# Two products of the identity ahead of each set of P's transposes, until the FFN begins

## The chip, the cores and the metric

The kernel runs on one core of one Trainium2 chip. A core has TensorE (matrix products, written into the banks of PSUM), VectorE, ScalarE, GpSimd and the queues that issue DMAs. The metric is the device time of one execution in microseconds. In the profile's rows TensorE is PE (its loads of weights PEld), VectorE is DVE, ScalarE is ACT, GpSimd is POOL, and SP issues DMAs.

## What is computed

Attention with a causal mask over blocks of 64 positions, for 8 batches of 8 heads with 576 positions of 64 columns, and behind it a feed-forward layer over the 4608 rows of the result:

```python
scores = scale * np.matmul(q, k.transpose(0, 1, 3, 2))
mask = (pos[:, None] // 64) >= (pos[None, :] // 64)
scores = np.where(mask, scores, -1000000000.0)
attn = np.exp(scores - scores.max(-1, keepdims=True))
attn = attn / (attn.sum(-1, keepdims=True) + 1e-09)
x = np.matmul(attn, v).transpose(0, 2, 1, 3).reshape(4608, 512)
h = x @ w_in                        # 512 x 2048
g = np.where(h >= 1, h, np.where(h <= -1, 0.0, (h + 1) ** 2 / 4))
out = g @ w_out                     # 2048 x 512
```

All of it is float32.

## The kernel before

**Split operands.** Operands are held in float32r, split into a high part and a low part (what the high part leaves over), so that a product is two or three products: scores are `qa`, `ka` and `qb`, `kb` (L482, L485), the FFN's first product is `wih` with `xh`, `wih` with `xl`, `wil` with `xh` (L770), its second is `gh` with two parts of w_out and `gl` with one (L794, L799). The parts of the weights are made while attention begins (`convert`, L156 to L189: ScalarE, VectorE and GpSimd in turn; VectorE's lines are L171, L174 and L177).

**Attention.** A pair of heads is one unit of work (`Pair`); there are 32, four to a batch. `scores` (L494) makes scores of 128 positions in a PSUM bank, VectorE takes their maximum (L505), ScalarE the exponential (L509), VectorE the reciprocal of the sum (L491, L492) and P (L515). `scores_last` (L518) does the same for the last 64 positions of both heads (L529 to L541). P must be transposed before it can be multiplied with V: `turn` (L556) and `turn_last` (L572) take a PSUM bank, transpose three or four pieces of 128x128 into it with TensorE (L554 for the first four pairs, L552 from the fifth on, when P has gone through a DMA first), and ScalarE copies the result out (L545). `weighted` (L587) multiplies it with V (L591); the result goes into `xh` and `xl` (L626, L627).

**Order of the work.** `attention_steps` (L663) is a generator of eight steps to a pair. The loop at L838 runs a step at a time, with pieces of the conversion of weights between them; from the 37th step on (`START` is 36, L830) it also runs a step of the FFN, and sets `banks["free"]` to False (L851). Until then `work_bank` (L80) takes every other bank from the four that the FFN's second product will use later. That written order is only the first word: a scheduler sets the order on each engine by priority and by its own estimate of times, and each engine takes its instructions in that order. So a set of transposes that waits for P holds back what stands behind it on TensorE.

Of the kernel before, what the change touches and what calls it, by code (L numbers as in the profile page):

```python
# [23 lines left out]
def block_attn_then_ffn(  # L24
# [9 lines left out]
    nc = tc.nc  # L34
# [25 lines left out]
    PLAIN = 2  # L60
    HOP = 1
    FAR = 2
    RAW = 2

    const = ctx.enter_context(tc.tile_pool(name="const", bufs=1))
# [12 lines left out]
    banks = {"free": True, "n": 0}  # L78

    def work_bank(name):  # L80

        banks["n"] += 1
        if banks["free"] and banks["n"] % 2:
            return ps_o.tile([P, 512], F32, tag="po", name=name)
        return ps_w.tile([P, 512], F32, tag="work", name=name)
# [4 lines left out]
    ident_r = const.tile([P, P], F32R, tag="ident", name="ident_r")  # L90
# [164 lines left out]
    class Pair:  # L255
# [4 lines left out]
        def __init__(self, b, hp):  # L260
# [6 lines left out]
            self.hop = b >= HOP  # L267
            self.raw = b >= RAW

            self.far = b >= FAR  # L270
            self.pr, self.nat = {}, {}
# [277 lines left out]
        def transposed(self, out, parts, c0, n):  # L549
# [3 lines left out]
            else:  # L553
                nc.tensor.transpose(out, src, ident)  # L554

        def turn(self, j, g):  # L556
            tiles = self.GROUPS[g]
            n = sum(t + 1 for t, _ in tiles) * P
            pr = self.pr.pop((j, g))
            ps = work_bank("ps_t")  # L560
            for c0 in range(0, n, P):
                self.transposed(ps[:, c0 : c0 + P], pr, c0, P)
            if g == 0:
                self.split(ps[:, :n], *self.pa[j])
            else:
                c0 = (g - 1) * P
                self.split(
                    ps[:, :n].rearrange("p (t c) -> p t c", c=P),
                    *(x[:, j, : n // P, c0 : c0 + P] for x in self.pb),
                )  # L570

        def turn_last(self):  # L572
            pr = self.pr.pop("last")
            ps = work_bank("ps_t")
            for c0 in range(0, SM, P):
                self.transposed(ps[:, c0 : c0 + P], pr, c0, P)
            self.split(
                ps[:, :SM].rearrange("p (t h c) -> p t h c", h=2, c=BLK),
                *(x[:, :, :, G1 - BLK :].rearrange("p h t c -> p t h c") for x in self.pb),
            )  # L580
            ps = work_bank("ps_t")
            self.transposed(ps[:BLK, :P], pr, SM, BLK)
            self.split(
                ps[:BLK, :P].rearrange("p (h c) -> p h c", h=2), *(x[:BLK] for x in self.pc)
            )
# [299 lines left out]
```

## Time and profile before

| | us |
|---|---|
| median of 3 runs | 1267.14 (1266.32 to 1267.73) |
| the profiled execution | 1269.69 |
| its span | 1267.9 |
| TensorE busy | 1200.1 |
| VectorE busy | 887.0 |
| ScalarE busy | 703.2 |
| GpSimd busy | 394.6 |

The span runs from the first to the last instruction of the profiled execution. Matmuls overlap, so the duration of one in a row is longer than the distance between two starts. "Idle" in square brackets of a row is the time in which the engine did nothing just before, with what ended it. PEclk is the granted clock of TensorE as a share of 2.4 GHz.

### The profile page before, as it was taken

Reading aid. Unit: us, or ns where it says so; the run is one execution under the profiler, and the core shown is the slowest. Engines: PE = TensorE matmul, PEld = TensorE weight load, DVE = VectorE, ACT = ScalarE, POOL = GpSimd, SP = SyncE. Lnnn points to the kernel's source line nnn. Section 1 sums busy time; section 2 is a strip of 40 time slices with the busy share of each in tenths; the row PEclk is TensorE's granted clock in tenths of the full one; section 3 lists DMA queues with packets and bytes.
Section 4 is the critical chain, followed back from the end, with each engine's and each line's share of the span. In section 5 each row is a group of like instructions: output and inputs, shape, how many; then the busy total and the mean of one; then the engine's idle time right before and its main releaser. Section 6 shows DMA issues by size and latency. Waiting matters only on the chain.

```text
span 1267.9 us, 20253 instructions
## 1 busy us (share of the span) xinstructions
PE 1200.1 (95%) x6280; PEld 998.8 (79%) x6280; DVE 887.0 (70%) x2188; ACT 703.2 (55%) x1827; POOL 394.6 (31%) x430
## 2 busy tenths in 40 slices
PE   5888889899999999999999999999999999999998
PEld 4666667678888888888888888888888888888886
DVE  8898877758777777777777777787777777322222
ACT  5787656646566655665656655566556555222222
POOL 3555655522222222222222222222222222222222
PEclk9888988999999999999999999999999999999999
DMA  5566666667888655555554655465556433422432
GB/s 158 167 176 215 203 228 197 217 198 237 260 273 266 215 162 158 154 175 163 156 162 145 187 157 152 138 189 153 160 154 190 137 128 118 132 87 98 133 100 100
DMA packets 185259, 215.43 MB, mean 170 GB/s; under 512 B 113840, under 2 KB 132272, under 8 KB 184384
## 3 DMA queue, kind: packets, MB, share of 16 engines
q1 hardware_dynamic: 185152, 214.14, 54.9%
q8 instruction: 50, 0.82, 0.3%
q14 instruction: 57, 0.47, 0.1%
HBM read 134.74 MB, written 31.98 MB: 131 GB/s over the span
## 4 chain that ended last, share of the span: by engine, by line
PE 69%; DVE 16%; ACT 6%; issue 5%; DMA 1%; POOL 1%; SPq 1%; ACTq 0%; POOLq 0%; DVEq 0%
PE ph L770 29%; PE po L794 15%; PE po L799 7%; PE ps_av L591 7%; PE ps_s L482 4%; ACT pr L509 3%; PE ps_s L485 3%; DVE t L780 2%; PE ps_t L552 2%; DVE t L783 2%; ACT t L779 2%; DVE pb L547 2%; DVE nm L505 2%; DVE sm L491 1%; DVE pr L515 1%
## 5 line engine op out<-in xcount | busy, mean ns | idle before, releaser
L785 POOL TENSOR_TENSOR gl<-t,gh 128x512 fp32r<-128x512 f32 x144 | 187.5, 1302 | 510.2 <-ACT gh L784 333.2
L794 PE MATMUL po<-wo,gh 128*128 128x512 f32 x1152 | 296.1, 397 | 0.5 <-DMA wo<-wo_split 0.3
L794 PEld LDWEIGHTS po<-wo,gh 128*128 128x128 f32 x1152 | 212.5, 189 | 44.5 <-DMA wo<-wo_split 0.7
L770 PE MATMUL ph<-xh,wih 128*128 128x512 f32 x576 | 232.9, 404 | 1.6 <-DVE t L783 1.6
L770 PE MATMUL ph<-xh,wil 128*128 128x512 f32 x576 | 228.8, 397 | 0.0
L770 PE MATMUL ph<-xl,wih 128*128 128x512 f32 x576 | 227.8, 396 | 0.5 <-DVE xl L627 0.5
L780 DVE SCALAR_TENSOR_TENSOR t<-t 128x512 f32<-128x512 f32 x144 | 101.5, 705 | 168.0 <-ACT t L779 165.2
L779 ACT ACTIVATE t<-ph 128x512 f32<-128x512 f32 x144 | 85.9, 597 | 173.8 <-PE ph L770 173.8
L509 ACT ACTIVATE pr<-ps_s,nm 128x128 f32<-128x128 f32 (+3 forms) x256 | 134.1, 527 | 60.5 <-DVE nm L505 58.4
L784 ACT CAST gh<-t 128x512 fp32r<-128x512 f32 x144 | 89.5, 621 | 120.3 <-DVE t L783 120.0
L799 PE MATMUL po<-wo,gl 128*128 128x512 f32 x576 | 155.6, 392 | 0.0
L482 PE MATMUL ps_s<-ka,qa 68*128 68x288 f32 (+4 forms) x384 | 135.3, 367 | 15.0 <-ACT pr L509 5.4
L379 POOL TENSOR_TENSOR vsr<-vn,vsr 128x256 fp32r<-128x256 f32 (+1 forms) x96 | 55.2, 576 | 246.2 <-ACT vsr L378 244.6
L770 PEld LDWEIGHTS ph<-xh,wil 128*128 128x128 f32 x576 | 109.5, 190 | 23.8
L770 PEld LDWEIGHTS ph<-xh,wih 128*128 128x128 f32 x576 | 109.8, 191 | 21.7 <-DVE t L783 2.3
L799 PEld LDWEIGHTS po<-wo,gl 128*128 128x128 f32 x576 | 108.7, 189 | 23.1
L505 DVE TENSOR_REDUCE nm<-ps_s 128x1 f32<-128x128 f32 (+3 forms) x256 | 118.8, 482 | 10.4 <-PE ps_s L485 9.4
L770 PEld LDWEIGHTS ph<-xl,wih 128*128 128x128 f32 x576 | 109.7, 190 | 20.5 <-DVE xl L627 0.9
L485 PE MATMUL ps_s<-kb,qb 128*128 128x288 f32 (+4 forms) x384 | 121.1, 322 | 0.0
L515 DVE TENSOR_SCALAR pr<-pr,sm 128x128 f32<-128x128 f32 (+3 forms) x256 | 107.3, 440 | 5.4
L783 DVE TENSOR_TENSOR t<-ph,t 128x512 f32<-128x512 f32 x144 | 98.7, 686 | 2.2
L491 DVE TENSOR_SCALAR sm<-sm 128x1 f32<-128x1 f32 (+1 forms) x224 | 52.0, 232 | 68.3 <-ACT pr L509 65.7
(111 smaller groups left out, 1871.4 us busy)
## 6 DMA issues: line engine op xcount, KB each, us to landing
wo<-wo_split SPq DMA_DIRECT2D x144, 512.0 KB, 3.5
prr<-pr SPq DMA_DIRECT2D x96, 192.0 KB, 2.5
prr<-pr SPq DMA_DIRECT2D x72, 256.0 KB, 2.8
out_dram<-ob SPq DMA_DIRECT2D x36, 256.0 KB, 2.9
bits<-in_moe_w_in_dram SPq DMA_DIRECT2D x32, 256.0 KB, 3.5
bits<-in_moe_w_out_dram SPq DMA_DIRECT2D x32, 256.0 KB, 3.0
wo_split<-ws SPq DMA_DIRECT2D x16, 512.0 KB, 2.9
qa<-qb SPq DMA_DIRECT2D x63, 128.0 KB, 2.4
```

The costliest lines, as they stand in the source:

```text
L482: nc.tensor.matmul(ps, qa[:KA, j, c0 : c0 + P], ka[:KA, j, k0 : k0 + n], start=first, stop=False)
L485: nc.tensor.matmul(ps, qb[:, j, c0 : c0 + P], kb[:, j, k0 : k0 + n], start=False, stop=last)
L505: nc.vector.tensor_reduce(out=nm[:, i : i + 1], in_=ps[:, cs], axis=AX.X, op=ALU.max, negate=True)
L509: nc.scalar.activation(pr[:, cs], ps[:, cs], AF.Exp, bias=nm[:, i : i + 1], scale=1.0, accum_out=sm[:, i : i + 1],)
L515: nc.vector.tensor_scalar_mul(pr[:, cs], pr[:, cs], sm[:, i : i + 1])
L770: nc.tensor.matmul(ph, w[:, cc, fs], x[:, cc, xs], start=(cc == 0 and i == 0), stop=(cc == NCC - 1 and i == 2),)
L779: nc.scalar.activation(t_, ph, AF.Relu, bias=0.5, scale=0.5)
L780: nc.vector.scalar_tensor_tensor(out=t_, in0=t_, scalar=1.0, in1=t_, op0=ALU.min, op1=ALU.mult)
L783: nc.vector.tensor_tensor(out=t_, in0=ph, in1=t_, op=ALU.max)
L785: nc.gpsimd.tensor_tensor(out=gl, in0=t_, in1=gh.bitcast(F32), op=ALU.subtract)
L794: nc.tensor.matmul(po[tt], gh[:, ts_], wo[:, w, :], start=(fc == 0 and w == 0), stop=False)
L799: nc.tensor.matmul(po[tt], gl[:, ts_], wo[:, 0, :], start=False, stop=fc == NFC - 1)
```

## The change

A method `dense` issues two products of the identity with itself into the PSUM bank that the transposes of P take next. The moving operand is the identity four times side by side (128x512), both products start a new sum, and the transposes write over the result. It is called in `turn` and `turn_last`, ahead of the transposes, as long as `banks["free"]` is true: for the first four pairs and three sets of the fifth, 31 sets or 62 products in all.

```diff
--- before.py
+++ after.py
@@ -60,6 +60,7 @@
     PLAIN = 2
     HOP = 1
     FAR = 2
+    DENSE = 2
     RAW = 2
 
     const = ctx.enter_context(tc.tile_pool(name="const", bufs=1))
@@ -553,11 +554,19 @@
             else:
                 nc.tensor.transpose(out, src, ident)
 
+        def dense(self, ps):
+
+            part, cols = ident_r.ap
+            moving = bass.AP(tensor=ident_r.tensor, offset=ident_r.offset, ap=[part, [0, 4], cols])
+            for _ in range(DENSE if banks["free"] else 0):
+                nc.tensor.matmul(ps, ident_r, moving, start=True, stop=True)
+
         def turn(self, j, g):
             tiles = self.GROUPS[g]
             n = sum(t + 1 for t, _ in tiles) * P
             pr = self.pr.pop((j, g))
             ps = work_bank("ps_t")
+            self.dense(ps)
             for c0 in range(0, n, P):
                 self.transposed(ps[:, c0 : c0 + P], pr, c0, P)
             if g == 0:
@@ -572,6 +581,7 @@
         def turn_last(self):
             pr = self.pr.pop("last")
             ps = work_bank("ps_t")
+            self.dense(ps)
             for c0 in range(0, SM, P):
                 self.transposed(ps[:, c0 : c0 + P], pr, c0, P)
             self.split(
```

The lines of the changed kernel stand lower by one from L63 on and by ten behind `turn_last`: the products of the identity are L562, the transposes L553 and L555, scores L483 and L486, P times V L601, the FFN's first product L780.

In the order of TensorE, the first pair of heads, before (the transposes L554 with 64x128 at their end are the last P's; the products L591 are P times V):

```order
L422 MATMUL ps_qk<-ident_r,qs 128x128 x4
L554 MATMUL ps_t<-ident_r,pr 128x128 x4
L554 MATMUL ps_t<-ident_r,pr 64x128
L422 MATMUL ps_qk<-ident_r,ks 128x128 x4
L482 MATMUL ps_s<-ka,qa 128x512
L485 MATMUL ps_s<-kb,qb 128x512
L554 MATMUL ps_t<-ident_r,pr 128x128 x3
L591 MATMUL ps_av<-pa_250,vs 128x256
L554 MATMUL ps_t<-ident_r,pr 128x128 x3
L591 MATMUL ps_av<-pa_250,vs 128x128
```

The same place in the changed kernel:

```order
L423 MATMUL ps_qk<-ident_r,qs 128x128 x4
L562 MATMUL ps_t<-ident_r 128x512 x2
L423 MATMUL ps_qk<-ident_r,ks 128x128 x4
L562 MATMUL ps_t<-ident_r 128x512 x2
L601 MATMUL ps_av<-pa_250,vs 128x256
L555 MATMUL ps_t<-ident_r,pr 128x128 x4
L555 MATMUL ps_t<-ident_r,pr 64x128
L483 MATMUL ps_s<-ka,qa 128x512
L486 MATMUL ps_s<-kb,qb 128x512
L555 MATMUL ps_t<-ident_r,pr 128x128 x3
L562 MATMUL ps_t<-ident_r 128x512 x2
L555 MATMUL ps_t<-ident_r,pr 128x128 x3
```

Two sets now stand ahead of the last P's transposes (L555 with 64x128 at their end), behind the transposes of Q and of K, and one between later transposes of P.

The second pair, before, from the end of the first three products of an FFN step on:

```order
L770 MATMUL ph<-xh,wil 128x512
L554 MATMUL ps_t<-ident_r,pr 128x128 x4
L554 MATMUL ps_t<-ident_r,pr 64x128
L422 MATMUL ps_qk<-ident_r,ks 128x128 x4
L482 MATMUL ps_s<-ka,qa 128x512
L485 MATMUL ps_s<-kb,qb 128x512
L554 MATMUL ps_t<-ident_r,pr 128x128 x3
L591 MATMUL ps_av<-pa_529,vs 128x256
L554 MATMUL ps_t<-ident_r,pr 128x128 x3
L591 MATMUL ps_av<-pa_529,vs 128x128
```

The same place in the changed kernel:

```order
L562 MATMUL ps_t<-ident_r 128x512 x2
L780 MATMUL ph<-xh,wih 128x512
L780 MATMUL ph<-xl,wih 128x512
L555 MATMUL ps_t<-ident_r,pr 128x128 x4
L555 MATMUL ps_t<-ident_r,pr 64x128
L423 MATMUL ps_qk<-ident_r,ks 128x128 x4
L483 MATMUL ps_s<-ka,qa 128x512
L486 MATMUL ps_s<-kb,qb 128x512
L562 MATMUL ps_t<-ident_r 128x512 x2
L555 MATMUL ps_t<-ident_r,pr 128x128 x3
L562 MATMUL ps_t<-ident_r 128x512 x2
L601 MATMUL ps_av<-pa_543,vs 128x256
```

The set of the last P stands ahead of two FFN products and of the transposes that it belongs to; two more sets follow among the later transposes of P.

## Rows read from the trace of the kernel before

**Rows 1.** From the page: engines' busy time, and the chain that ended last.
```profile
PE 1200.1 (95%) x6280; PEld 998.8 (79%) x6280; DVE 887.0 (70%) x2188; ACT 703.2 (55%) x1827; POOL 394.6 (31%) x430
...
PE 69%; DVE 16%; ACT 6%; issue 5%; DMA 1%; POOL 1%; SPq 1%; ACTq 0%; POOLq 0%; DVEq 0%
```

**Rows 2.** Table by stretches: busy us (instructions) of each engine, PEclk, DMA share, GB/s.
```profile
12.00:33.00 21.00, 16.44 (x67) 13.79 (x68) 18.40 (x59) 16.12 (x50) 10.30 (x12) 1.00 0.57 158
...
50.00:57.00 7.00, 6.64 (x30) 5.87 (x30) 5.87 (x19) 3.62 (x11) 4.07 (x5) 0.53 0.58 166
...
70.00:77.00 7.00, 5.17 (x21) 4.37 (x22) 6.60 (x23) 4.56 (x16) 3.66 (x5) 0.52 0.39 112
77.00:101.00 24.00, 19.80 (x130) 16.12 (x129) 22.86 (x72) 21.91 (x66) 15.99 (x20) 1.00 0.70 207
101.00:104.00 3.00, 3.00 (x7) 1.83 (x7) 3.00 (x14) 3.00 (x13) 0.05 (x1) 0.50 0.91 335
...
115.00:118.00 3.00, 3.00 (x8) 2.30 (x7) 2.86 (x8) 1.08 (x3) 1.35 (x2) 0.50 0.51 169
...
180.00:280.00 100.00, 88.69 (x392) 68.19 (x391) 69.73 (x173) 55.59 (x157) 45.98 (x58) 0.88 0.65 207
280.00:1268.00 988.00, 968.67 (x5158) 816.62 (x5157) 663.59 (x1579) 521.28 (x1301) 254.45 (x253) 1.00 0.53 162
```

**Rows 3.** Waits of TensorE up to 118 us: total us, times, longest.
```profile
PE ps_t L554 <- DVE sm L491: 7.5, 3, 3.8
...
PE ps_t L554 <- DVE pr L515: 3.9, 5, 1.5
...
PE ps_t L554 <- ACT pr L535: 1.6, 1, 1.6
PE ps_t L554 <- ACT pr L509: 1.5, 1, 1.5
PE ps_t L552 <- DMA vsr<-pr: 1.4, 1, 1.4
```

**Rows 4.** VectorE in order of time: start, us, what [idle before it and releaser].
```profile
29.19 0.69 DVE L505 TENSOR_REDUCE nm<-ps_s 128x1 f32<-128x512 f32 x1 [0.92 <-PE ps_s L485]
...
33.94 0.43 DVE L627 TENSOR_TENSOR xl<-ps_av,xh 128x256 fp32r<-128x256 f32 x1 [1.92 <-ACT xh L626]
...
53.14 0.69 DVE L505 TENSOR_REDUCE nm<-ps_s 128x1 f32<-128x512 f32 x1 [0.33 <-PE ps_s L485]
...
57.30 0.42 DVE L627 TENSOR_TENSOR xl<-ps_av,xh 128x256 fp32r<-128x256 f32 x1 [0.71 <-ACT xh L626]
...
76.26 0.69 DVE L505 TENSOR_REDUCE nm<-ps_s 128x1 f32<-128x512 f32 x1 [0.33 <-PE ps_s L485]
...
108.08 0.49 DVE L627 TENSOR_TENSOR xl<-ps_av,xh 128x320 fp32r<-128x320 f32 x1 [1.40 <-ACT xh L626]
```

**Rows 5.** TensorE in order of time, same columns: transposes of P.
```profile
26.40 1.30 PE L554 MATMUL ps_t<-ident_r,pr 128*128 128x128 f32 x5 [2.08 <-DVE sm L491]
...
50.36 1.30 PE L554 MATMUL ps_t<-ident_r,pr 128*128 128x128 f32 x5 [3.76 <-DVE sm L491]
...
73.48 1.30 PE L554 MATMUL ps_t<-ident_r,pr 128*128 128x128 f32 x5 [1.63 <-DVE sm L491]
...
92.98 0.74 PE L554 MATMUL ps_t<-ident_r,pr 128*128 128x128 f32 x5 [1.46 <-ACT pr L509]
...
99.92 0.63 PE L554 MATMUL ps_t<-ident_r,pr 128*128 128x128 f32 x4 [1.47 <-DVE pr L515]
```

**Rows 6.** TensorE in order of time: products of the FFN, at two clocks.
```profile
89.16 0.40 PE L770 MATMUL ph<-xl,wih 128*128 128x512 f32 x1
89.39 0.40 PE L770 MATMUL ph<-xh,wil 128*128 128x512 f32 x1
...
115.88 0.63 PE L770 MATMUL ph<-xl,wih 128*128 128x512 f32 x1
116.31 0.63 PE L770 MATMUL ph<-xh,wil 128*128 128x512 f32 x1
```

## The prediction

> **What bounds the kernel now.** I read the page first. TensorE is busy for 95% of the span, and the chain of work that ended last runs through it for 69% and through VectorE for 16% [rows 1]. That mean covers two stages, so next came the table by stretches [rows 2]. From 280 us to the end TensorE is busy 968.67 of 988 us at clock 1.00: there every microsecond of TensorE counts, and the change puts nothing there. Before the FFN it is otherwise. From 77 to 101 us VectorE is busy 22.86 of 24 us and TensorE 19.80: VectorE sets the pace, and TensorE waits for it. Third, the waits of TensorE in this stage: ahead of the transposes it waits 7.5, 3.9, 1.6, 1.5 and 1.4 us, together 15.9 us, nearly all for P from VectorE or ScalarE [rows 3]. Fourth, VectorE's own gaps, for only a gap there can be won: 0.92 and 1.92 us in the first pair of heads, 0.33 and 0.71 in the second, 0.33 in the third, 1.40 in the fourth [rows 4], together 5.61 us. Each stands behind a long run of TensorE (the last P's transposes, scores, P times V).
>
> Those runs go at half clock. The stretches 50 to 57, 70 to 77, 101 to 104 and 115 to 118 us have a granted clock of 0.53, 0.52, 0.50 and 0.50 [rows 2], where 0.50 is 1.2 of 2.4 GHz. Ahead of the second pair's run the engine had waited 3.76 us, ahead of the third's 1.63 us [rows 5]. For the first pair the column reads 1.00, but the durations say otherwise: five transposes take 1.30 us at 26.40 us, the same 1.30 us as at 50.36 and 73.48 us in stretches recorded at half clock, and 0.74 us at 92.98 us, where it is full [rows 5]. So I take the first run to be at half clock too. The Trainium skill (TensorE: Matmul & The Clock Gate, Part 1, HAM trace caveats) says that recorded clock events on trn2 have been seen to be unreliable. Here the trace agrees: a clock of 1.00 beside durations of half clock.
>
> **The change part by part.** It adds 62 products of 128x512, two ahead of each of 31 sets of transposes: seven sets for each of the first four pairs, three for the fifth. Nothing is removed. The trace has a like product, a line of the FFN's first product: its starts are 89.16 and 89.39 us, 0.23 us apart, at full clock, and 115.88 and 116.31 us, 0.43 us apart, at half [rows 6]. A set then costs 0.46 us at full clock and 0.86 us at half, all 31 of them 14.3 to 26.7 us of TensorE. Each product waits for nothing but its PSUM bank, so that a set whose transposes wait for P runs within that wait. The cover is the 15.9 us [rows 3]; without it the whole 14.3 us would be on the path. The two places of the order show where the cover is missing: of the first pair's run one set, between transposes whose P is there, and of the second pair's run two.
>
> What the sets may give back is the clock of the runs, and of that no more than VectorE's gaps behind them. By place:
>
> First pair, the run from 26.40 us. In the new order two sets stand ahead of the last P's transposes, where 2.08 us were idle [rows 5], and one set more, one that is split into two single products, and a third lie among the scores before them. If this brings full clock before the run, it takes half as long, and both gaps (0.92 + 1.92 = 2.84 us) close, less one uncovered set, 0.46: 2.4 us won. If it stays at half clock, the set costs 0.86. I take the gain, since the engine is given work in just those gaps, and full clock doesn't ask for a row without gaps: from 77 to 101 us it stays 1.00 with 19.80 of 24 us busy [rows 2].
>
> Second pair, from 50.36 us. One set and two FFN products now stand in the 3.76 us wait; some 2.9 us of it stay idle, still more than any other wait of [rows 5], so I let the clock fall as before. Ends: full clock closes 0.33 + 0.71 = 1.04 us; half clock throughout costs two sets, 1.72 us. With a rise part of the way through, about the middle: 0.3 us lost.
>
> Third pair, from 73.48 us: waits of 1.63 us, each now with a set in it. Ends: 0.33 us won (VectorE has no more to give), or one uncovered set at half clock, 0.86 lost. I take 0.3 won.
>
> Fourth pair, from 99.92 us: half clock is recorded from 101 us, after a wait of 1.47 us [rows 5], in which a set now runs at no cost. Ends: 1.40 us won, or nothing. I take 1.4 won, since that wait was the last idle time ahead of the fall, and 0.46 us of it are filled.
>
> Fifth pair and the FFN's first products, 108 to 118 us. Of three sets one lies in the 1.4 us wait for a DMA [rows 3]; two cost 0.92 us, and no wait covers them. Products from 115 to 118 us ran at half clock; at full clock 3.0 us become 1.5. Ends: 0.6 won, 1.7 lost (two sets at half clock). I take 0.6 won, for the set in the wait stands right ahead of them.
>
> Sum: -2.4 + 0.3 - 0.3 - 1.4 - 0.6 = -4.4 us. VectorE's, ScalarE's and the queues' work stays the same in amount; conversions of weights change places with reductions of scores on VectorE here and there, which I cost at nothing, since VectorE is full on both sides of the exchange; if a reduction stands behind one conversion more where TensorE waits, that is some 0.4 us each. The profiled execution took 1269.69 us, its span 1267.9; the runs' median is 1267.14, 2.6 us below. The difference goes onto the median: 1262.7 us.
>
> **The rivals.** No change: VectorE gives back only its gaps, and if the first run stays at half clock, the sum is +0.9 + 0.3 - 0.3 - 1.4 + 0.9 = +0.4 us, 1267.5 us. For it: VectorE is 95% busy from 77 to 101 us [rows 2]. Against it: 2.84 us of gaps in the first pair alone.
>
> Slower: the sets themselves run at half clock inside the runs. A set of 0.46 us is small beside an idle time of 3.76 us, and if it wakes nothing, each uncovered set costs 0.86: 0.9 + 1.7 + 0.9 in the first three pairs, 1.7 in the fifth, nothing won: 5.2 us, 1272.3 us. It decides as soon as two of the runs stay at half clock to their end. For it: the second run was busy for 6.64 of 7.00 us and its clock stayed low for most of that [rows 2]. Against it: 77 to 101 us, where a TensorE with 4.2 us of gaps in 24 keeps full clock.
>
> Transposes don't count: the chip's clock is held by products alone, and runs that begin with transposes stay at half clock, as the first three do, while the fourth and fifth, which are products, are held: 0.9 + 1.7 + 0.9 - 1.4 - 0.6 = +1.5 us, 1268.6 us. The Trainium skill states this rule (TensorE: Matmul & The Clock Gate, Part 4): full clock does not engage for transposes. Against it: from 77 to 101 us, with P's transposes in many places, the clock stays 1.00 [rows 2].
>
> Much faster: from 180 to 280 us the clock averages 0.88 [rows 2], which is 12 us of engine time. The change puts nothing there, but shifts it all, and falls may drop out; half of them would be 6 us more, 1257 us. They may as well be added to, so this is a spread and not a gain.
>
> That the sets don't do what they say: the scheduler pulls some away from their transposes (of the first pair two sets are split into single products among the scores, which still fill gaps); it is part of the no-change case.
>
> **How the numbers follow.** Forecast 0.44, much faster 0.11, no change 0.21, transposes don't count 0.07, slower 0.17. Within 0.2% is 2.5 us either way, about what a measurement can tell: 1264.6 to 1269.7. The forecast and the much faster case are faster: 0.55. No change and most of the transposes' case are within: 0.27. The slower case and the rest: 0.18. The likeliest is 1262.7 us. The range goes down to the much faster case and up to most of the slower one: 1257.0 to 1270.5 us.
>
> **What would show it.** Right: in the first pair five transposes of the last P take about 0.74 us instead of 1.30, VectorE's gaps of 0.92 and 1.92 us are gone, and the stretches at 101 and 115 us are at 1.00. The second pair's stretch may be at half clock still. The FFN's products that stand at 115.88 us [rows 6] begin some 4 us earlier. Wrong: five transposes of 1.30 us in the first three pairs and larger gaps on VectorE behind them (the slower case), or all runs at full clock and the FFN begun 4 us earlier, but the lead lost between 120 and 280 us, with more falls of the clock there.

## The result, and the profile after

The changed kernel takes 1272.15 us (median of 6 runs, 1270.30 to 1274.01) beside 1267.92 us of the kernel before (6 runs, 1266.32 to 1269.81): ratio 1.0033, 95% interval 1.0021 to 1.0046. It is slower by about 4 us. 1262.7 us and a faster kernel were forecast. The profiled execution took 1274.01 us, its span 1272.2.

The page of the changed kernel, engines' busy time and the chain that ended last, as [rows 1]:

```profile
PE 1210.4 (95%) x6342; PEld 1008.5 (79%) x6342; DVE 891.0 (70%) x2188; ACT 704.4 (55%) x1827; POOL 392.1 (31%) x430
...
PE 69%; DVE 8%; ACT 5%; issue 3%; POOL 1%; DMA 1%; SPq 0%; ACTq 0%; POOLq 0%; DVEq 0%
```

TensorE has 62 products more (6342 for 6280) and is busy 10.3 us longer; the other engines have the same instructions. From the ninth pair of heads on both kernels need the same: its scores begin at 270.5 us before and at 274.8 after, and 997.4 us remain in both profiles. So the time was lost ahead of it, and the table by stretches is the place to look. First the kernel before, in six stretches (columns as in [rows 2]):

```profile
33.00:57.00 24.00, 18.86 (x99) 15.11 (x97) 21.87 (x65) 18.13 (x57) 13.56 (x17) 0.86 0.63 186
57.00:77.00 20.00, 16.19 (x86) 12.94 (x86) 18.57 (x57) 15.54 (x49) 9.33 (x12) 0.83 0.53 148
...
101.00:118.00 17.00, 14.91 (x60) 11.09 (x60) 15.00 (x47) 10.18 (x34) 7.20 (x10) 0.80 0.59 190
118.00:180.00 62.00, 53.98 (x282) 42.66 (x281) 49.09 (x117) 40.88 (x113) 36.10 (x42) 1.00 0.69 220
```

The stretches 77 to 101 and 180 to 280 us of it are in [rows 2]. The changed kernel:

```profile
33.00:57.00 24.00, 21.35 (x123) 17.16 (x121) 22.66 (x67) 20.20 (x62) 13.17 (x18) 0.93 0.61 183
57.00:77.00 20.00, 16.21 (x74) 11.90 (x73) 19.01 (x57) 13.18 (x43) 11.70 (x15) 0.86 0.52 165
77.00:101.00 24.00, 20.51 (x111) 16.86 (x110) 20.67 (x61) 18.27 (x56) 10.47 (x15) 0.86 0.61 181
101.00:118.00 17.00, 17.00 (x98) 13.84 (x97) 15.22 (x44) 11.68 (x35) 8.12 (x11) 0.97 0.61 181
118.00:180.00 62.00, 50.12 (x224) 38.89 (x223) 43.77 (x114) 37.80 (x106) 31.91 (x39) 0.84 0.61 197
180.00:280.00 100.00, 90.59 (x449) 72.40 (x449) 77.23 (x178) 62.13 (x170) 50.44 (x61) 0.96 0.71 221
```

Read the clock column first. One minus the clock, times the stretch, is the engine time that half clock costs. From 33 to 280 us that is 22.2 us before and 22.3 us after: the falls have not gone, they stand elsewhere. From 77 to 101 us and from 118 to 180 us, where the kernel before has 1.00, the changed one has 0.86 and 0.84; it wins in the others. VectorE from 77 to 101 us is busy 20.67 us, and 22.86 before [rows 2]: the stretch that VectorE set the pace of now has waits of VectorE too.

Those stretches cut the pairs at different places, so here is the same from the start of the second pair's scores to the start of the fifth's, VectorE alone: in each case a row of all its instructions, and a row of its conversions of weights (those on `work`). The columns are the stretch, its length, busy us (instructions), and then clock and DMA as above. First before, then after:

```profile
33.26:97.75 64.49, 60.15 (x185) 0.89 0.61 179
33.26:97.75 64.49, 22.48 (x56) 0.89 0.61 179
...
32.70:105.73 73.03, 66.52 (x196) 0.88 0.58 177
32.70:105.73 73.03, 29.37 (x63) 0.88 0.58 177
```

The three pairs take 8.5 us longer. VectorE's idle time makes 2.2 us of that (6.5 for 4.3); for the other 6.4 us it is busy, and its conversions of weights alone take 6.9 us more: there are seven more of them, and each takes 0.47 us where it took 0.40. From the fifth pair to the ninth, where fewer conversions are left, 3.6 us come back (169.1 us for 172.7).

TensorE's waits up to 118 us, as [rows 3]:

```profile
PE ps_t L555 <- DVE pr L516: 5.6, 3, 2.6
PE ps_t L562 <- ACT pr L510: 2.4, 1, 2.4
...
PE ps_t L555 <- DVE pr L542: 0.4, 1, 0.4
```

The 7.5 us for the last P are gone from it, but 5.6 us for a P of VectorE stand in their place (3.9 before). VectorE's larger gaps, as [rows 4]:

```profile
29.96 0.69 DVE L506 TENSOR_REDUCE nm<-ps_s 128x1 f32<-128x512 f32 x1 [0.95 <-PE ps_s L486]
...
33.38 0.42 DVE L637 TENSOR_TENSOR xl<-ps_av,xh 128x256 fp32r<-128x256 f32 x1 [0.54 <-ACT xh L636]
...
78.48 0.69 DVE L506 TENSOR_REDUCE nm<-ps_s 128x1 f32<-128x512 f32 x1 [1.09 <-PE ps_s L486]
80.08 0.15 DVE L492 TENSOR_SCALAR sm<-sm 128x1 f32<-128x1 f32 x1 [0.90 <-ACT pr L510]
```

The 1.92 us of the first pair have shrunk to 0.54, and the 0.71 and 1.40 us of [rows 4] are gone. But the 0.92 us are still 0.95, and behind the third pair's run 0.33 has become 1.09 us, with 0.90 more next to it. Over all, VectorE's waits from 14 to 118 us add up to 7.7 us, and to 7.6 before: they have moved. TensorE's transposes of P and two sets of products, as [rows 5, 6]:

```profile
27.80 1.27 PE L555 MATMUL ps_t<-ident_r,pr 128*128 128x128 f32 x5
...
49.48 1.33 PE L555 MATMUL ps_t<-ident_r,pr 128*128 128x128 f32 x5 [0.42 <-DVE pr L542]
...
76.40 1.27 PE L555 MATMUL ps_t<-ident_r,pr 128*128 128x128 f32 x5
...
92.73 0.63 PE L562 MATMUL ps_t<-ident_r 128*128 128x512 f32 x2
95.91 1.12 PE L555 MATMUL ps_t<-ident_r,pr 128*128 128x128 f32 x4 [2.55 <-DVE pr L516]
...
98.06 1.05 PE L562 MATMUL ps_t<-ident_r 128*128 128x512 f32 x2
```

The five transposes go at half clock in all of the first three pairs (1.27 to 1.33 us); behind them the second run is soon at full clock (its scores of 128x512 at 51.33 us take 0.40 us). And at 95.91 us, a place where the kernel before was at full clock, a wait of 2.55 us comes first and half clock follows. What VectorE did there, in order of time:

```profile
88.53 0.48 DVE L172 TENSOR_SCALAR work<-work 128x256 f32<-128x256 f32 x2
88.94 2.31 DVE L175 TENSOR_SCALAR work<-work 128x256 uint32<-128x256 uint32 x2
91.17 0.41 DVE L178 SCALAR_TENSOR_TENSOR work<-work 128x256 uint32<-128x256 uint32 x1
91.61 0.49 DVE L637 TENSOR_TENSOR xl<-ps_av,xh 128x320 fp32r<-128x320 f32 x1
92.02 0.68 DVE L506 TENSOR_REDUCE nm<-ps_s 128x1 f32<-128x512 f32 x1
```

and the same place of the kernel before:

```profile
86.43 0.48 DVE L171 TENSOR_SCALAR work<-work 128x256 f32<-128x256 f32 x2
86.83 0.28 DVE L174 TENSOR_SCALAR work<-work 128x256 uint32<-128x256 uint32 x1
87.15 0.69 DVE L505 TENSOR_REDUCE nm<-ps_s 128x1 f32<-128x512 f32 x1
87.76 0.48 DVE L627 TENSOR_TENSOR xl<-ps_av,xh 128x320 fp32r<-128x320 f32 x1
```

Two instructions of conversions more (a second L175 and an L178) now stand ahead of the maximum and `xl`. From the first L175 to `xl` 2.67 us pass; the one L174 before took 0.28 us, the two L175 take 2.31, of which 2.12 are the first of them and 0.27 the second. While the first ran, GpSimd had a difference of two operands in SBUF, and two MEMSETs behind it:

```profile
88.74 1.56 POOL L365 TENSOR_TENSOR ks<-kn,ks 128x576 fp32r<-128x576 f32 x1 [0.85 <-DVE ks L364]
90.24 0.66 POOL L315 MEMSET vs<- 128x320 f32 x2
```

The Trainium skill (SBUF — State Buffer, Summary: rules for kernel authors) says that of GpSimd and a VectorE in a two-port mode the one that issues second is blocked until the first has finished. The trace agrees so far: the conversion that starts at 88.94 us, behind GpSimd's start at 88.74, is the one that is stretched, and it ends at 91.05, just behind the MEMSETs. Whether it ran in such a mode no run here shows. So the price of a conversion that is moved forward isn't the 0.4 us that I gave it.

### The profile page after: what moved, and what is told of

The parts are those of the page before. It is cut to its first block, busy times and chain, and to the rows that moved or that the text cites. A ratio compares the mean times of both kernels' runs of the same rounds, so it can differ in the third digit from the quotient of the medians.

```text
span 1272.2 us, 20353 instructions
## 1 busy us (share of the span) xinstructions
PE 1210.4 (95%) x6342; PEld 1008.5 (79%) x6342; DVE 891.0 (70%) x2188; ACT 704.4 (55%) x1827; POOL 392.1 (31%) x430
## 4 chain that ended last, share of the span: by engine, by line
PE 69%; DVE 8%; ACT 5%; issue 3%; POOL 1%; DMA 1%; SPq 0%; ACTq 0%; POOLq 0%; DVEq 0%
PE ph L780 29%; PE po L804 15%; PE po L809 8%; PE ps_av L601 6%; PE ps_s L483 4%; PE ps_s L486 3%; PE ps_t L553 2%; ACT pr L510 2%; DVE t L790 2%; DVE t L793 2%; ACT t L789 1%; DVE pb L548 1%; PE ps_qk L402 1%; DVE sm L492 1%; DVE x L624 1%
## 5 line engine op out<-in xcount | busy, mean ns | idle before, releaser
L780 PE MATMUL ph<-xh,wih 128*128 128x512 f32 x576 | 232.4, 403 | 1.9 <-DVE sm L492 1.9
L780 PE MATMUL ph<-xh,wil 128*128 128x512 f32 x576 | 228.1, 396 | 0.0
L780 PE MATMUL ph<-xl,wih 128*128 128x512 f32 x576 | 226.9, 394 | 0.0
L483 PE MATMUL ps_s<-ka,qa 68*128 68x288 f32 (+4 forms) x384 | 134.0, 364 | 8.1 <-ACT pr L510 5.3
L780 PEld LDWEIGHTS ph<-xh,wil 128*128 128x128 f32 x576 | 109.3, 190 | 23.8
L780 PEld LDWEIGHTS ph<-xh,wih 128*128 128x128 f32 x576 | 109.5, 190 | 21.4 <-DVE sm L492 2.0
L780 PEld LDWEIGHTS ph<-xl,wih 128*128 128x128 f32 x576 | 109.8, 191 | 19.6
L486 PE MATMUL ps_s<-kb,qb 128*128 128x288 f32 (+4 forms) x384 | 120.9, 322 | 0.0
L516 DVE TENSOR_SCALAR pr<-pr,sm 128x128 f32<-128x128 f32 (+3 forms) x256 | 102.6, 422 | 6.0 <-DVE sm L493 0.6
```

The lines of the kernel that those rows point to most:

```text
L483: nc.tensor.matmul(ps, qa[:KA, j, c0 : c0 + P], ka[:KA, j, k0 : k0 + n], start=first, stop=False)
L486: nc.tensor.matmul(ps, qb[:, j, c0 : c0 + P], kb[:, j, k0 : k0 + n], start=False, stop=last)
L516: nc.vector.tensor_scalar_mul(pr[:, cs], pr[:, cs], sm[:, i : i + 1])
L780: nc.tensor.matmul(ph, w[:, cc, fs], x[:, cc, xs], start=(cc == 0 and i == 0), stop=(cc == NCC - 1 and i == 2),)
```

## The experiments

All are made by one device. The program is built without the products, which gives the kernel before with its order on each engine; then it is built again with them, and each instruction of an engine in `ONLY` is tied behind its predecessor of the first order. Where TensorE's order is kept, a set of products stays just ahead of its transposes. What is not in `ONLY` the scheduler orders anew. In the traces every engine that is kept has the old order, instruction for instruction.

```diff
+    ONLY = None                      # None: every engine
+        for queue in (q_ for e, q_ in order.items() if ONLY is None or e in ONLY):
+            for x, y in zip(queue, queue[1:]):
+                after(own[y], own[x])
...
+    order = build(Sets(lambda b, hp, s: 0))[2]
+    nc, arrays, _ = build(Sets(lambda b, hp, s: 512), order)
```

Ratios are to the kernel before on the same chip, with the 95% interval; each changed kernel was run 5 to 12 times, the kernel before 6 to 29 times beside it.

| run | order kept | products | median us | ratio |
|---|---|---|---|---|
| the changed kernel | none | 62 | 1272.15 | 1.0033 (1.0021 to 1.0046) |
| order_alone | all of the changed kernel's | 62 of 16 columns | 1272.91 | 1.0036 (1.0022 to 1.0049) |
| work_old_order | all five | 62 | 1265.51 | 0.9980 (0.9968 to 0.9992) |
| one_old_order | all five | 31 | 1266.63 | 0.9991 (0.9980 to 1.0001) |
| four_old_order | all five | 124 | 1270.00 | 1.0013 (1.0004 to 1.0022) |
| waits_old_order | all five | 26 | 1267.26 | 0.9994 (0.9982 to 1.0005) |
| old_order_three_pairs | all five | 44 | 1267.44 | 1.0001 (0.9984 to 1.0017) |
| old_order_two_pairs | all five | 28 | 1266.55 | 0.9992 (0.9978 to 1.0006) |
| only_tensor_order_new | all but TensorE | 62 | 1265.28 | 0.9989 (0.9977 to 1.0002) |
| gpsimd_order_new | all but GpSimd | 62 | 1265.32 | 0.9985 (0.9972 to 0.9998) |
| queue_order_new | all but SP | 62 | 1268.76 | 1.0007 (0.9995 to 1.0018) |
| scalar_order_new | all but ScalarE | 62 | 1270.93 | 1.0029 (1.0016 to 1.0041) |
| vector_order_new | all but VectorE | 62 | 1273.62 | 1.0051 (1.0037 to 1.0065) |
| only_tensor_order_old | TensorE | 62 | 1274.95 | 1.0055 (1.0043 to 1.0067) |
| vector_order_old | VectorE | 62 | 1269.67 | 1.0023 (1.0008 to 1.0039) |
| tensor_vector_order_old | TensorE, VectorE | 62 | 1275.78 | 1.0070 (1.0047 to 1.0092) |
| vector_scalar_order_old | VectorE, ScalarE | 62 | 1278.34 | 1.0086 (1.0068 to 1.0105) |
| vector_scalar_gpsimd_order_old | VectorE, ScalarE, GpSimd | 62 | 1275.63 | 1.0064 (1.0051 to 1.0077) |
| vector_scalar_queue_order_old | VectorE, ScalarE, SP | 62 | 1267.63 | 0.9996 (0.9985 to 1.0008) |

**The products, or the order?** Two runs part the change in its halves. The first has all its work and the old order; its edit is the device above.

> All 62 products of 128x512, and every other instruction of every engine pinned to the order of the kernel before; a set stands directly ahead of its own transposes. Theory 'work' (the products take some 14 us of TensorE, of which the idle time and the clock give back only a part): slower by 3 to 5 us, as the changed kernel. Theory 'order' (the products are covered, and the loss comes from the scheduler's new order): within 1.5 us of the kernel before. Theory of the prediction (the sets wake the clock, the new order spoils it): 3 to 5 us faster.

The second has the changed kernel's order on every engine, the products included, and cuts each product to 16 of 512 columns (the products' results are written over in any case).

```diff
-    WHOLE = False
+    WHOLE = True                     # the products keep their places too
...
-    order = build(Sets(lambda b, hp, s: 0))[2]
-    nc, arrays, _ = build(Sets(lambda b, hp, s: 512), order)
+    order = build(Sets(lambda b, hp, s: 512))[2]
+    nc, arrays, _ = build(Sets(lambda b, hp, s: 16), order)
```

> The order of the changed kernel on every engine, its 62 products included, but each product cut to 16 columns, so that it takes next to no time on TensorE and fills no gap. Theory 'work': within 1.5 us of the kernel before. Theory 'order': slower by 3 to 5 us. Theory of the prediction with a spoiling order: slower by more than the changed kernel, since the clock's gain is gone and the order stays: 6 us or more.

The answer is plain: the order alone makes the kernel slower by 0.36%, as much as the whole change (0.33%); the work alone makes it faster by 0.20%. No theory fits both runs as written: the order alone is 5 us slower, as 'order' has it, but the work alone is 2.3 us faster, between 'order' and the prediction's own theory. In the new order the work wins nothing that can be told (1.0033 with it, 1.0036 without). The old order tied down without any product was not run; the runs below with fewer products, all within 0.1% of the kernel before, speak against a gain from the tying itself. In the old order the clock does what the change can bring:

```profile
33.00:57.00 24.00, 20.85 (x132) 17.22 (x131) 21.80 (x66) 20.59 (x63) 13.70 (x17) 1.00 0.63 187
57.00:77.00 20.00, 18.66 (x113) 15.08 (x113) 19.29 (x63) 17.54 (x56) 12.08 (x15) 1.00 0.62 182
77.00:101.00 24.00, 21.88 (x127) 17.37 (x128) 23.80 (x72) 20.31 (x65) 13.39 (x17) 1.00 0.66 202
101.00:118.00 17.00, 15.70 (x77) 12.24 (x76) 15.50 (x45) 10.96 (x33) 8.69 (x11) 0.90 0.57 187
118.00:180.00 62.00, 53.77 (x268) 42.41 (x267) 48.92 (x118) 40.68 (x113) 36.50 (x43) 0.94 0.69 221
180.00:280.00 100.00, 86.49 (x400) 67.20 (x399) 68.00 (x168) 54.62 (x152) 43.33 (x55) 0.94 0.65 205
```

From 33 to 101 us it is 1.00 throughout, and half clock costs 11.4 us from 33 to 280 us where it cost 22.2. In TensorE's rows of this run the waits are still there, and the clock is held through them:

```profile
27.65 0.74 PE L556 MATMUL ps_t<-ident_r,pr 128*128 128x128 f32 x5 [1.78 <-DVE sm L493]
...
50.87 0.74 PE L556 MATMUL ps_t<-ident_r,pr 128*128 128x128 f32 x5 [3.15 <-DVE sm L493]
...
70.37 0.74 PE L556 MATMUL ps_t<-ident_r,pr 128*128 128x128 f32 x5 [0.89 <-DVE pr L543]
```

**How many products, and where?** One and four instead of two to a set, then two ahead of only those sets that wait the longest:

```diff
-    DENSE = 2
+    DENSE = 1        # one_old_order; four_old_order has 4
```

> One product to a set, 31 in all, every order pinned to that of the kernel before. Two to a set were 2.3 us faster than before and four 2.2 us slower. If one is enough to hold the clock before the FFN, the products cost 7 us less of TensorE, and the sum is 3 to 5 us faster than before. If it isn't, the clock falls in the second and third pair as before, and the sum is within 1.5 us of before.

> Four products to a set instead of two, 124 in all, the rest pinned to the order of the kernel before. Theory 'work': the second two of a set find less idle time than the first two, so the loss against the kernel before more than doubles that of two to a set: 9 to 16 us slower. Theory 'order': under 3 us slower. Theory of the prediction: the clock stays at its full level before the FFN, and the sum is 2 to 6 us faster than before.

```diff
+    nc, arrays, _ = build(Sets(lambda b, hp, s: 512 if s in ("02", "last", "12") else 0), order)
```

> Two products ahead of three of a pair's seven sets alone, those before which TensorE waited for P in the kernel before (the third group of the first head, the last positions, the third group of the second head); 26 products, every order pinned to that of the kernel before. If the gain comes from work in those waits: 3 to 5 us faster than before, more than with all sets, since the uncovered ones are gone. If it takes work in all places to hold the clock: within 1.5 us.

One to a set is no longer told from no change; the falls at 47.8 and 71.7 us stay. Four is slower. Products at the waits alone gain nothing that can be told either: a fall at 47.7 us stays.

The next two leave the products in the first three pairs (and one set of each later pair), and in the second and third pair alone, since with all of them the fourth took 2.4 us longer than before, where the clock had been full anyway:

```diff
+    nc, arrays, _ = build(Sets(lambda b, hp, s: 512 if (b == 0 and hp < 3) or s == "12" else 0), order)
```

> Every order kept as in the kernel before; the products stand only ahead of the sets of the first three pairs of batch 0 and of each pair's set 12, 44 in all. In the run with all 62 products and the old order, pair 3 (79 to 98 us before) lost 2.4 us to products that no wait covered, with no clock to win there. If uncovered products are pure cost, this is 3 to 5 us faster than the kernel before. If the products of the later pairs also hold the clock there, it is 1 to 2.5 us faster, no better than with all of them.

```diff
+    nc, arrays, _ = build(Sets(lambda b, hp, s: 512 if b == 0 and hp in (1, 2) else 0), order)
```

> Every order kept as in the kernel before; the products stand only in pairs 1 and 2 of batch 0 (33 to 79 us), where the clock fell in the kernel before and did not with the products. If what the products bring is the clock of these two pairs, this keeps it all and pays for 16 sets or fewer: 3 to 5 us faster than before. If the gain needs the later pairs or the first one too, within 1 us of before.

"Uncovered products are pure cost" falls. With hardly a product in the fourth pair it takes the same 21.0 us as with all (18.6 before), VectorE idle for 0.2 of them in both. The pair is paced by VectorE: from the second pair to the fourth VectorE is idle 4.3 us before and 1.8 us with the products in either number, and the three pairs take 2.3 us less in both (one trace each). With products in the second and third pair alone a fall comes back at 50.2 us. Neither run is told from no change, nor from work_old_order, and both miss the 3 to 5 us that were hoped for.

**Which engine's order?** Two first runs: only TensorE's order kept, and all but TensorE's.

```diff
+    ONLY = ['EngineType.PE']
```

> 62 products of 128x512; TensorE's order pinned to that of the kernel before, the other engines' and queues' order left to the scheduler, which changes them in many places, as in the changed kernel. If the loss of the changed kernel lies in VectorE's, ScalarE's, GpSimd's and the queues' order (theory 'others'): 2 to 5 us slower than before. If it lies in TensorE's own order (theory 'TensorE'): 1 to 3 us faster, as with all orders pinned.

```diff
+    ONLY = ['EngineType.DVE', 'EngineType.Activation', 'EngineType.Pool', 'EngineType.SP']
```

> 62 products of 128x512; VectorE, ScalarE, GpSimd and the queues pinned to the order of the kernel before, TensorE's order left to the scheduler. Theory 'others': 1 to 3 us faster than before. Theory 'TensorE': 2 to 5 us slower.

TensorE's own order is not the loss: new and alone it costs nothing that can be told, and kept alone it saves nothing (7.4 us slower, beyond the 2 to 5 of theory 'others'). My next theory was VectorE's order.

```diff
+    ONLY = ['EngineType.DVE']          # tensor_vector_order_old: 'EngineType.PE' too
```

> All 62 products of the change; VectorE's instructions keep the order of the kernel before, TensorE, ScalarE, GpSimd and the transfers are ordered anew by the scheduler. If VectorE's order alone carries the loss (conversions of weights moved ahead of the copies and reductions that others wait for), this is faster than the kernel before by 1 to 3 us, near the 1265.5 of the run with every order kept. If the loss comes from the order on ScalarE, GpSimd or the queues, it is slower by 2 to 5 us, as the changed kernel is.

> All 62 products; TensorE's and VectorE's instructions keep the order of the kernel before, ScalarE, GpSimd and the transfers are ordered anew. With VectorE as the cause: 1 to 3 us faster than before. With ScalarE, GpSimd or the queues as the cause: 2 to 7 us slower, as the run with only TensorE's order kept was.

That theory fell in this form: to keep VectorE's order, with TensorE's or without, does not save the change. So I freed one engine at a time, with the others in the old order (the edit for VectorE; the other three likewise):

```diff
+    ONLY = ['EngineType.PE', 'EngineType.Activation', 'EngineType.Pool', 'EngineType.SP']   # VectorE free
```

> All 62 products; TensorE, ScalarE, GpSimd and the transfers keep the order of the kernel before, VectorE alone is ordered anew. If VectorE's order carries the loss by itself, 2 to 5 us slower than before. If it is ScalarE's, GpSimd's or the transfers' order, 1 to 3 us faster, as with every order kept. If the loss needs the order of several engines to change together, also near 1265.5.

> All 62 products; ScalarE alone is ordered anew, every other engine keeps the old order. If ScalarE's order carries the loss (roundings of weights ahead of exponentials and copies that VectorE and TensorE wait for), 2 to 5 us slower than before; with another engine as the cause, or several together, 1 to 3 us faster.

> All 62 products; GpSimd alone is ordered anew. GpSimd's differences feed ScalarE's roundings, which wait for them 10 us in this stretch. If GpSimd's order carries the loss, 2 to 5 us slower than before; otherwise 1 to 3 us faster.

> All 62 products; the transfers that SP issues alone are ordered anew (quarters of weights ahead of the copies of q and k between partitions). If their order carries the loss, 2 to 5 us slower than before; otherwise 1 to 3 us faster.

With the products' gain in them, the runs are 0.51% slower for VectorE's new order and 0.29% for ScalarE's. The transfers' new order takes the gain away (1.0007, where every order kept has 0.9980; the intervals lie apart), which neither of the two theories had. The run for GpSimd tests little: left free, only 2 of its 430 instructions leave their places, where in the changed kernel about 69 do. It is nearly work_old_order once more, and repeats its gain (0.9985). In the run with VectorE free, TensorE's wait for the second pair's last P is 4.22 us where it was 3.15 with the old order, and half clock follows it:

```profile
54.45 1.30 PE L556 MATMUL ps_t<-ident_r,pr 128*128 128x128 f32 x5 [4.22 <-DVE sm L493]
```

If those two orders were all, keeping both would be enough:

```diff
+    ONLY = ['EngineType.Activation', 'EngineType.DVE']
```

> All 62 products; VectorE and ScalarE keep the order of the kernel before, TensorE, GpSimd and the transfers are ordered anew. If the loss is the new order on VectorE and ScalarE, and keeping only one of them failed because the other was still new: 1 to 3 us faster than before, near the 1265.5 of every order kept. If the transfers or GpSimd also bring a loss when TensorE's order is new too: 1 to 3 us slower, as with VectorE's order alone kept.

A miss: 1.0086, the slowest of all. Its trace had ScalarE waiting 11.7 us for quarters of weights from memory from 85 to 280 us, so the last two runs add one more engine each:

```diff
+    ONLY = ['EngineType.DVE', 'EngineType.Activation', 'EngineType.SP']     # the second: 'Pool' for 'SP'
```

> All 62 products; VectorE, ScalarE and the transfers on SP keep the order of the kernel before, TensorE and GpSimd are ordered anew. If late transfers made the loss of the run without SP's order, 1 to 3 us faster than before. If it was GpSimd's order, 3 to 10 us slower. If both were needed, in between.

> All 62 products; VectorE, ScalarE and GpSimd keep the order of the kernel before, TensorE and the transfers on SP are ordered anew. If late transfers made the loss, 5 to 10 us slower than before. If it was GpSimd's order, 1 to 3 us faster.

It is the transfers. With SP's order kept the loss is gone (0.9996; no gain is left, though 1 to 3 us were expected), with GpSimd's it stays (1.0064). Where it stays, SP in order of time (only the stretch ahead of the late weights):

```profile
159.95 0.38 SPq L802 DMA_DIRECT2D wo<-wo_split  x1
160.42 0.69 SPq L435 DMA_DIRECT2D qa<-qb  x1
163.77 0.47 SPq L245 DMA_DIRECT2D prs<-pr  x1
164.29 2.41 SPq L166 DMA_DIRECT2D bits<-in_moe_w_in_dram  x3
```

and all engines behind it:

```profile
168.23 0.43 ACT L171 ACTIVATE work<-bits 128x256 f32<-128x256 f32 x1 [6.91 <-DMA bits<-in_moe_w_in_dram]
168.70 0.29 DVE L173 TENSOR_SCALAR work<-work 128x256 f32<-128x256 f32 x1 [4.96 <-ACT work L171]
...
169.51 0.54 PE L424 MATMUL ps_qk<-ident_r,ks 128*128 128x128 f32 x4 [2.00 <-ACT pb L547]
```

The three loads of `bits` stand behind a copy of P (`prs`), for which the queue waits 2.6 us until VectorE has P. The loads start at 164.29 us, ScalarE idles 6.91 us, VectorE 4.96. This is a part of the loss only: by the fifth pair's scores this run is 5.1 us behind the one with SP's order kept already (99.5 and 94.4 us). With SP's order kept, the same place has one load ahead of the copy of q:

```profile
151.86 0.55 SPq L166 DMA_DIRECT2D bits<-in_moe_w_in_dram  x1
153.16 0.48 SPq L435 DMA_DIRECT2D qa<-qb  x1
```

and ScalarE's longest wait for these weights from 118 to 180 us is 1.8 us. In the changed kernel itself this wait is not among ScalarE's larger ones. So VectorE's and ScalarE's orders are the likeliest causes there, since each costs by itself; that is argued and not shown. How much of the 0.36% each engine carries in the changed kernel stays open: what the scheduler gives a freed engine is not the order that it has there (about 76 of VectorE's instructions leave their places when it alone is free, about 353 in the changed kernel), and the changed kernel's order on one engine beside the old one on the others was not tried, since the two wait for each other.

## Why the prediction was wrong

**The step that failed** is one clause: "conversions of weights change places with reductions of scores on VectorE here and there, which I cost at nothing, since VectorE is full on both sides of the exchange", with 0.4 us each as its worst. Order alone, with the products cut to next to nothing, costs 0.36%, some 5 us, as much as the whole forecast gain. That VectorE is full makes the exchange dear and not free: where it sets the pace, a conversion that is moved in lengthens the pair. From the second pair to the fourth the changed kernel has 63 of them for 56, and VectorE is busy 6.4 us longer; order_alone has the same 63, and takes 74.5 us for these pairs where the kernel before takes 64.5. Nor is VectorE full on both sides any more: its idle time in these pairs grows by 2.2 us. A result that TensorE needs stands behind conversions, TensorE waits, its clock falls behind the wait, and VectorE then waits for TensorE. And two conversions did not cost 0.4 us each, but 2.31 together. The exchanges also reach ScalarE and SP, of which I said that their work "stays the same in amount": true, and no argument on the order. The new order was priced on TensorE alone.

**The mechanism was right, and the sum too large.** With every order kept the products gain 0.2% (0.1 to 0.3), 2.5 us where 4.4 were forecast. TensorE's account up to the scores of the ninth pair splits the time of one profile each into idle time (with all that lies ahead of the first scores, 12 to 13 us), half clock (half of the busy time in stretches at half clock) and the rest. In the profiles the records of the clock begin only at 32.8, 20.2 and 22.0 us (before, changed, work_old_order); ahead of that the clock column reads 1.00 for want of a record, and not, as the prediction took it, by a wrong one. The durations there are those of half clock (128x512 in 0.63 us), so the time up to the first record is counted as half clock:

| us | idle | half clock | the rest | ninth pair begins |
|---|---|---|---|---|
| before | 50.9 | 28.3 | 191.3 | 270.5 |
| the changed kernel | 45.8 | 26.3 | 202.7 | 274.8 |
| work_old_order | 45.8 | 17.1 | 205.0 | 267.9 |

The cover is the term that was too large. I took the waits of 15.9 us [rows 3] to hide nearly all of the sets. In either order only 5 us of idle time went, and the rest of TensorE's time grew by 11.4 and 13.7 us (62 products at 0.23 us are 14.3). So the products are paid for with half clock, if it goes: 11.2 us in the old order, 2.0 in the new one.

By start of each pair's scores, in the profiled runs of before and of work_old_order:

| term | forecast us | in the old order |
|---|---|---|
| first pair | -2.4 | +0.9 (second pair begins at 34.2, was 33.3; 0.5 of it lies ahead of the first scores) |
| second | +0.3 | -2.5 (21.6 us, was 24.1) |
| third | -0.3 | -2.3 (19.5, was 21.8) |
| fourth pair of heads | none | +2.4 (21.0, was 18.6) |
| fourth and fifth runs (fifth pair) | -2.0 | -1.4 (28.9, was 30.3) |

The first pair failed: the five transposes do come to 0.74 us and the gap of 0.92 us is gone, as foreseen, but half clock begins at 28.8 us, right behind them, and VectorE still waits 2.13 us for `xh`. The second was better than I let it be: the wait of 3.15 us behind a set does not lower the clock. The fourth gives back what was won, for VectorE is the limit that I named, and only its gaps could be won: 2.5 us of idle time are all that it gave up over three pairs.

**Of the rivals** the slower one came out in its time (1272.3 forecast, 1272.15 measured), but not by its mechanism. It said that the sets, being too little to wake the clock, leave the runs at half clock; with the same sets in the old order the second and third run are at full clock. "Transposes don't count" has the same runs against it: the runs that begin with transposes are at full clock in the old order (rows of 27.65, 50.87 and 70.37 us). The Trainium skill's rule (TensorE: Matmul & The Clock Gate, Part 4) could still hold for transposes with no product near them; no run here shows those alone. Of the sentence on what would prove me wrong, the first half came true (1.27 to 1.33 us in all three pairs, VectorE's gaps behind them 0.95, 0.41 and 1.09 us for 0.92, 0.33 and 0.33), though not by the cause that I gave it: in the other order the same sets hold the clock. That the slower rival's time was met is luck.

## What to carry to other kernels

Where a scheduler sets the order, a change that adds instructions to one engine is two changes, the work and a new order on all engines, and the second can be the larger. Time them apart: keep the old order with the new work, and the new order with work cut to nothing. Before costing a move at zero, ask whether the engine sets the pace where the instruction lands, whose result now stands behind it, and whether that engine's wait has a price of its own, as TensorE's has in its clock.

The version with the old order and all 62 products (0.9980, interval 0.9968 to 0.9992) beats both kernels.

## What the runs showed of the hardware

A wait of 3.15 us behind a set of two products left the clock at 1.00 at 50.87 us; in the kernel before a wait of 3.76 us at the same place was followed by half clock, and with VectorE's order free one of 4.22 us behind a set was too. The length of the wait does not settle it: in the changed kernel half clock is recorded from 47.5 us on, behind a wait of 2.23 us that ended at 46.35. And a VectorE instruction of 0.28 us was stretched to 2.12 us beside GpSimd's difference of 1.56 us and two MEMSETs, so that what a moved instruction costs depends on what it lands beside.
